# Gates carried behind the rows of x, a routing pass moved by two steps, and four weight pieces split earlier, in a kernel of windowed attention and top-1 experts

## The chip, the cores and the metric

The kernel runs as one program on one core of a Trainium2 chip. The metric is the device time of one execution in microseconds. Three runs of the kernel before took 633.39, 634.94 and 635.16 us; the median is 634.94.

## The reference

q, k and v have 8 batches, 8 heads, 576 positions and a head dimension of 64. Each position attends to itself and to earlier positions: in heads 0 to 3 to the nearest 32, in heads 4 to 7 to every fourth within 128. The outputs of the heads, side by side, give x with 4608 rows of 512. A top-1 mixture of 8 experts follows; row by row the one chosen expert is applied.

```python
scores = where(mask[head], q @ k.T / 8, -1e9)          # 8 x 8 x 576 x 576
attn   = exp(scores - max); attn /= attn.sum() + 1e-9
x      = (attn @ v) as [4608, 512]
logits = x @ w_gate                                     # [4608, 8]
idx    = argmax(logits); gate = softmax(logits)[idx]
for e in range(8):
    rows = idx == e
    out[rows] = gate[rows] * (relu(x[rows] @ w1[e]) @ w2[e])   # 512 -> 1024 -> 512
```

## The kernel before

**Attention** goes in 36 steps: four pairs of batches (m = 0 to 3), nine tiles of 128 rows each. It is a software pipeline: step n computes the scores, maxima and exponentials of tile n, transposes the probabilities of tile n-1 on TensorE (ACT copies them to `pts`), multiplies those of tile n-2 with v (DVE divides the sums out, `xs`, and POOL writes the rows to `x_d` in DRAM), transposes x of tile n-3 and computes the routing logits of tile n-4. The functions are `st_scores`, `st_max` (L304), `st_sub` (L309), `st_trans` (L325), `st_ptcopy` (L330), `st_av` (L340), `st_z` (L350), `st_x` (L360) and `st_xout` (L372, L382); `step` calls them. Up to step 34 (`MEND` = 35) the instructions of TensorE, DVE and ACT keep the order of the code; POOL and SyncE, and all engines from step 35 on, are ordered by the scheduler.

**Routing.** When a pair's last logits exist, at its ninth step plus 4, `route(m)` puts some forty small pieces of work on a list called `side`: turning the logits, the maximum, the gate's softmax, the rank of each row among its expert's rows (three matmuls, `rank`, L520), its place (`select`, L528, to L626), and nine scatters. `step` takes pieces from the list's head at fixed points, `pull_pe` those for TensorE and `pull_off` those for the other engines. A scatter computes nine times 128 addresses `at_i` on DVE (L534) and writes, by an indirect DMA that POOL issues (L540), each row's number, and in the pairs 0 to 2 its gate, into a table with 80 places per partition. There are three tables, taken in turn, which SyncE reads back and POOL adds (L672 to L674). Pair 3, which has no scatters of this kind ahead of the experts, adds its own part by matmuls (`mark`), and DVE makes the sum: the final row list, L444, `row_i`. Pair 3's gates follow by nine scatters of their own into three further tables `gtab`, which `all_gates` reads, adds (L682 to L684) and writes to DRAM as `pairs`.

**The experts.** Blocks of 128 rows are gathered from `x_d` by the row list (POOL, L752). For experts 0 and 1 TensorE turns a block (`tpx`, L846), ACT copies the high part of x and DVE computes the low part (L853). For later experts the block goes back to DRAM (`put`) and returns in four DMAs (`quarters`, L772) in an arrangement that DVE can transpose. The last two dynamic blocks (`Tail`) gather 32 rows as 128 quarter rows and need one transpose. Weights arrive as `raw` (SyncE, L874) in three buffers and are split in a high and a low part, `wu`: ACT copies (L726), DVE subtracts (L727). During attention ACT (L738) and POOL (L741) do this for expert 0, one piece per step from the list `spare`. After the second layer (L926) ACT multiplies with the gate (`y`, L794) and POOL scatters the rows to the output (L795).

Expert 0's first rows come from pairs 0 and 1 alone, so its blocks are gathered and turned in the last attention steps, and its first layer starts there.

Of the kernel before, what the change touches and what calls it, by code (L numbers as in the profile page):

```python
# [23 lines left out]
N = B * S  # L24
# [27 lines left out]
QD = 32  # L52
NQ = P // QD
# [18 lines left out]
def _constants():  # L72
# [48 lines left out]
    slots = np.zeros((P, NBK, 2), np.int32)  # L121
    slots[:, :, 0] = np.arange(P)[:, None]
    slots = slots.reshape(P, 2 * NBK)
    return dict(cst=c, tok=tok, end=end, slots=slots, mask=mask, zero=np.zeros((DUMMY, 2 * NBK), np.float32))
# [39 lines left out]
def attention_moe_kernel(ctx, tc, qk, v, wg, w, cst, tok, end, slots, mask, zero, out):  # L164
# [14 lines left out]
    pair = const.tile([P, NBK + 1, 2], I32, name="pair")  # L179
    row_i, gall = pair[:, :NBK, 0], pair[:, :NBK, 1].bitcast(F32)  # L180
    base = const.tile([P, NBK], F32, name="base")
    first_i = const.tile([P, EB], I32, name="first_i")
    first_g = const.tile([P, EB], F32, name="first_g")
    last_i = [const.tile([P, NT], I32, name=f"last_i{i}") for i in range(2)]
    last_f = [const.tile([P, NT], F32, name=f"last_f{i}") for i in range(2)]
# [7 lines left out]
    dsp = ctx.enter_context(tc.tile_pool(name="dsp", bufs=1))  # L193

# [7 lines left out]
    t_in = [late.tile([P, NBK, 2], I32, name=f"t_in{i}") for i in range(3)]  # L202
# [23 lines left out]
    nc.gpsimd.memset(pair[:, NBK], 0)  # L226
# [15 lines left out]
    def load_rest():  # L242
        nc.sync.dma_start(cc, cst[:, C_ATT:])
        nc.sync.dma_start(rows_i, tok)
        nc.sync.dma_start(rows_f, end)
        for i, tab in enumerate(tabs):
            nc.sync.dma_start(
                tab[:].rearrange("(p b) o -> p (b o)", p=P), zero.bitcast(I32) if i else slots
            )

    def clear_rows():
        nc.sync.dma_start(x_d[:DUMMY], zero[:, :DM])
        nc.sync.dma_start(out[:DUMMY], zero[:, :DM])
        for tab in gtabs:
            nc.sync.dma_start(tab[:].rearrange("(p b) o -> p (b o)", p=P), zero[:, :NBK])
# [112 lines left out]
    def st_xout(n):  # L368
# [7 lines left out]
        while at < (t + 1) * P:  # L376
# [4 lines left out]
            rows = x_d[lo : lo + S, DM // 2 :].rearrange("(r j) d -> j r d", j=DIL)  # L381
# [72 lines left out]

    def pull_pe(late=False):
        if side and side[0][0] == (2 if late else 1) and (
# [8 lines left out]
    def pull_off():  # L465
        ticks[0] += 1
        if side and not side[0][0]:
            ticks[1] = ticks[0]
            side.pop(0)[1]()

    def route(m, then=None, after=None):
# [38 lines left out]
        load = small("load", (P, NT, 2), I32)  # L510
        if m == NPR - 1:
            (blk_i, at_i), (wide, gate) = last_i, last_f
# [33 lines left out]

        def scatter_gate(t):
            scatter(t, gtabs, gate[:, t : t + 1])
# [19 lines left out]
        def enter(ts):  # L568
# [3 lines left out]
            for t in ts:  # L572
# [49 lines left out]
        if m < NPR - 1:  # L622
            off_both(
                lambda: v.tensor_tensor(load[:, :, 0], rows_i[:, m], plc_i, op=ALU.subtract),
                lambda: v.tensor_copy(load[:, ::3, 0], rows_i[:, m, ::3]),
# [3 lines left out]
            def enter_pair():  # L629
                v.tensor_tensor(crun, crun, cs[:, :, NT - 1], op=ALU.add)  # L630
                for t in range(NT):
                    spaced(scatter, t, tabs, load[:, t])
# [4 lines left out]
        else:  # L637
# [17 lines left out]
            off_pe(v.tensor_tensor, row_i, t_in[0][:, :, 0], scr, op=ALU.add)  # L655
# [6 lines left out]
    gates_later = []  # L662

    def read_table(n):

        for tab, to in zip(tabs, t_in):
            nc.sync.dma_start(to[:, :n], tab[:].rearrange("(p b) o -> p b o", p=P)[:, :n])

    def add_tables(rows, gates, n):
# [1023 lines left out]
```

## Time and profile before

| what | value |
|---|---|
| median of three runs | 634.94 us (633.39 to 635.16) |
| the profiled execution | 631.91 us |
| its span | 630.1 us |
| TensorE's mean granted clock | 0.972 |
| TensorE busy | 596.9 us, 95% |
| DVE, ACT, POOL busy | 364.2, 315.5, 196.3 us |
| bytes moved | 153.40 MB, 243 GB/s in the mean |

The profile is of one execution. Busy times are sums over instructions; a TensorE that is busy may still run at a lower granted clock, so its busy share and its clock have to be read together, slice by slice. The attention steps end at about 172 us, expert 0 and the hand-over to the expert loop take until about 232 us, and the loop with its dynamic blocks fills the rest.

### The profile page before, as it was taken

How to read it: one execution, taken by the hardware profiler on the slowest of the kernel's cores; microseconds unless marked ns; L12 is line 12 of the kernel's file. 1: busy time of each engine (PE TensorE's matmuls, PEld its weight loads, DVE VectorE, ACT ScalarE, POOL GpSimd, SP SyncE). 2: the span in 40 equal slices, each digit the busy share in tenths (PEclk: the TensorE clock that was granted, in tenths of full speed). 3: DMA queues.
4: the chain of work that ended last, by engine and by line, in shares of the span. 5: the costliest groups of instructions: out<-in, count | busy, mean ns of one | idle time of the engine just before them, and what ended most of it. 6: DMA issues, size and time to landing. Idle time of an engine off the chain costs nothing. (4 is left out here: it accounts for less than half of the span.)

```text
span 630.1 us, 13462 instructions
## 1 busy us (share of the span) xinstructions
PE 596.9 (95%) x5175; PEld 484.7 (77%) x5175; DVE 364.2 (58%) x786; ACT 315.5 (50%) x606; POOL 196.3 (31%) x245
## 2 busy tenths in 40 slices
PE   7999999999799989999999999999999999999990
PEld 6878877767687768888888888888888888887770
DVE  3778878867558375645565656466665646652000
ACT  2677667667423455534564465356545645552100
POOL 0343375588744646230013011201401120120020
PEclk7999999989899989999999999999999999999996
DMA  8999999976235437986578778687877878696410
GB/s 335 411 400 412 411 407 398 338 240 199 70 97 176 129 135 272 262 271 211 163 237 289 198 230 285 224 246 237 281 211 221 275 252 218 219 325 240 150 40 21
DMA packets 64034, 153.40 MB, mean 243 GB/s; under 512 B 11184, under 2 KB 27440, under 8 KB 63920
## 3 DMA queue, kind: packets, MB, share of 16 engines
q1 hardware_dynamic: 52176, 123.05, 57.9%
q0 software_dynamic: 11792, 29.48, 13.7%
q8 instruction: 41, 0.67, 0.5%
q14 instruction: 25, 0.20, 0.1%
HBM read 125.26 MB, written 29.23 MB: 245 GB/s over the span
## 5 line engine op out<-in xcount | busy, mean ns | idle before, releaser
L926 PE MATMUL yps<-wu,h 128*128 128x512 f32 x696 | 166.4, 394 | 0.0
L727 DVE TENSOR_TENSOR wu<-raw,wu 128x512 fp32r<-128x512 f32 x200 | 128.8, 690 | 64.0 <-ACT wu L726 57.9
L895 PE MATMUL hps<-x,wu 128*128 128x512 f32 (+1 forms) x720 | 163.3, 385 | 0.2 <-DVE h L907 0.2
L895 PEld LDWEIGHTS hps<-x,wu 128*128 128x128 f32 x720 | 132.5, 188 | 28.9 <-DVE h L907 0.4
L926 PEld LDWEIGHTS yps<-wu,h 128*128 128x128 f32 x696 | 129.4, 188 | 29.1 <-issue 0.8
L726 ACT CAST wu<-raw 128x512 fp32r<-128x512 f32 x200 | 112.3, 618 | 5.6 <-DMA raw<-in_w_dram 5.6
L795 POOL DMA_INDIRECT out_dram<-y,pair x30 | 29.7, 990 | 193.8 <-ACT y L794 127.5
L907 DVE SCALAR_TENSOR_TENSOR h<-hps,h 128x512 fp32r<-128x512 f32 (+1 forms) x60 | 40.2, 671 | 58.5 <-ACT h L906 53.8
L330 ACT COPY pts<-pt 96x512 f32<-96x512 f32 x72 | 41.9, 582 | 54.9 <-PE pt L325 42.8
L906 ACT ACTIVATE h<-hps 128x512 fp32r<-128x512 f32 (+1 forms) x60 | 35.0, 583 | 63.4 <-PE hps L895 52.0
L752 POOL DMA_INDIRECT xg<-x_d,pair x30 | 31.9, 1062 | 102.2 <-DVE x L790 55.7
L304 DVE TENSOR_REDUCE nm<-s 128x4 f32<-128x384 f32 x72 | 39.5, 549 | 29.8 <-PE s L293 19.2
L325 PE MATMUL pt<-ident,p 128*96 128x128 f32 x288 | 48.5, 294 | 3.7 <-ACT pts L330 3.1
L340 PE MATMUL o<-vr,pts 96*64 96x65 f32 x1152 | 45.4, 232 | 2.1 <-issue 1.9
L340 PEld LDWEIGHTS o<-vr,pts 96*64 96x64 f32 x1152 | 39.7, 143 | 9.5 <-issue 8.3
L794 ACT ACTIVATE y<-yps,pair 128x512 f32<-128x512 f32 x28 | 19.3, 688 | 50.6 <-PE yps L926 29.4
L372 POOL DMA_DIRECT2D x_d<-xs x36 | 20.5, 570 | 71.8 <-DVE xs L360 30.9
L309 DVE TENSOR_TENSOR d<-s,nm 128x384 f32<-128x384 f32 x72 | 40.0, 557 | 4.6
L995 PE MATMUL hpd<-wu,xd 128*128 128x512 f32 x168 | 41.7, 403 | 0.0
L319 ACT ACTIVATE p<-d 128x384 f32<-128x384 f32 x72 | 37.5, 524 | 6.9 <-DVE d L309 6.9
L1027 PE MATMUL ypd<-wu,hd 128*128 128x512 f32 x168 | 41.0, 393 | 0.0
L325 PEld LDWEIGHTS pt<-ident,p 128*96 128x96 f32 x288 | 29.6, 131 | 11.9 <-ACT pts L330 4.8
(172 smaller groups left out, 642.8 us busy)
## 6 DMA issues: line engine op xcount, KB each, us to landing
raw<-in_w_dram SPq DMA_DIRECT2D x104, 512.0 KB
qkr<-in_qk_dram SPq DMA_DIRECT2D x36, 576.0 KB
vr<-in_v_dram SPq DMA_DIRECT2D x36, 520.0 KB
rows<-xg SPq DMA_DIRECT2D x29, 256.0 KB
xg<-rows SPq DMA_DIRECT2D x116, 64.0 KB
wu<-in_w_dram SPq DMA_DIRECT2D x12, 512.0 KB
x_d<-xs POOLq DMA_DIRECT2D x44, 128.0 KB
wz<-in_w_dram SPq DMA_DIRECT2D x4, 512.0 KB
```

Source lines behind the costliest of these rows:

```text
L304: nc.vector.tensor_reduce(st["nm", n][:, g], st["s", n][g], axis=AX.X, op=ALU.max)
L309: nc.vector.tensor_tensor(st["d", n][:, g], st["s", n][g], st["nm", n][:, g].broadcast_to([P, HP, KB]), op=ALU.subtract,)
L325: nc.tensor.transpose(pt[:KB, h], st["p", n][:, g, h], ident)
L330: nc.scalar.copy(st["pts", n][:, g], st.pop(("pt", n))[:KB])
L340: nc.tensor.matmul(st["o", n][QB * j : QB * (j + 1), g, h], lhsT=pts[:, g, h, QB * j : QB * (j + 1)], rhs=vr[:KB, n % NRV, a : a + DH + 1] ...
L726: nc.scalar.copy(u[:, 0, sl], raw[:, sl])
L727: nc.vector.tensor_tensor(u[:, 1, sl], raw[:, sl], u[:, 0, sl].bitcast(F32), op=ALU.subtract)
L895: nc.tensor.matmul(hps[:, : self.ns], lhsT=u[:, wpart, fs], rhs=self.x[:, xpart, c, : self.ns], start=(k == 0), stop=(k == 11),)
L907: nc.vector.scalar_tensor_tensor(h[:, 1, :n], hps[:, :n], 0.0, h[:, 0, :n].bitcast(F32), op0=ALU.max, op1=ALU.subtract,)
L926: nc.tensor.matmul(yps, lhsT=self.h[f][:, hpart, ts], rhs=u[:, wpart, fs], start=f == 0 and k == 0, stop=f == 7 and k == 2,)
L995: nc.tensor.matmul(hps, lhsT=self.x[:, xpart, c], rhs=u[:, wpart, ns], start=(k == 0), stop=(k == 11),)
L1027: nc.tensor.matmul(self.yps, lhsT=self.h[f // 4][:, hpart, f % 4], rhs=u[:, wpart, fs], start=f == 0 and k == 0, stop=f == 7 and k == 2,)
```

## The change

**Gates as columns.** A row of `x_d` grows from 512 to 528 numbers. Each pair's gates are copied 16 times side by side (`many`) and written behind the rows by one DMA that POOL issues. Every gathered row then brings its gate along: ACT copies it out of the block, or, where the block comes by quarters, a fifth small DMA loads it. Tables and row list carry the row number alone; the `gtab` tables, `all_gates`, the part of `add_tables` for the gates and `pairs` are gone, and SyncE writes the row list to DRAM (`keep_rows`). The two `Tail` blocks gather whole rows and transpose them in four pieces of 32 partitions.

**The hold.** When the gates of pair 2 are done, `hold(True)` stops `pull_pe` and `pull_off` until step 36, so the rest of pair 2's routing is taken up after the last scores and maxima.

**The splits.** The first four weight pieces of expert 0 are loaded at steps 6, 8, 10 and 12 and enter `spare` at steps 8 to 14; before, they were loaded at 24 to 30 and entered at 26 to 32. Each stands for two entries of `spare`.

```diff
+XP = DM + 16
-    x_d = dram.tile([N + DUMMY, DM], F32, name="x_d")
-    tabs = [dram.tile([P * NBK, 2], I32, name=f"tab{i}") for i in range(3)]
-    pairs = dram.tile([P * (NBK + 1), 2], I32, name="pairs")
-    gtabs = [dram.tile([P * NBK, 1], F32, name=f"gtab{i}") for i in range(3)]
+    x_d = dram.tile([N + DUMMY, XP], F32, name="x_d")
+    tabs = [dram.tile([P * NBK, 1], I32, name=f"tab{i}") for i in range(3)]
+    table = dram.tile([P * (NBK + 1), 1], I32, name="table")
...
+    def held():
+        return held_[0] and now[0] < total
...
     def pull_pe(late=False):
+        if held():
+            return
...
     def pull_off():
         ticks[0] += 1
-        if side and not side[0][0]:
+        if not held() and side and not side[0][0]:
...
             lambda: v.reciprocal(
-                load.bitcast(F32)[:, :, 1] if m < NPR - 1 else gate, se2
+                gate, se2
             ),
-        )
+            lambda: v.tensor_copy(many, gate.broadcast_to([P, NT, XP - DM])),
+            lambda: nc.gpsimd.dma_start(
+                x_d[DUMMY + m * S2 : DUMMY + (m + 1) * S2, DM:].rearrange("(t p) o -> p t o", p=P),
+                many,
+            ),
+        )
+        if m == NPR - 2:
+            off_pe(hold, True)
         on_pe(rank, late=True)
...
-            off_pe(lambda: v.tensor_scalar_mul(wide, posf, float(NBK)))
-            for t in range(NT):
-                gates_later.append(lambda t=t: scatter_gate(t))
...
+    def gate_of(xg):
+        gate = gates.tile([P, 1], F32, name="gate")
+        return gate, nc.scalar.copy(gate, xg[:, DM : DM + 1])
...
     def quarters(rows):
...
+        nc.sync.dma_start(gate, rows[:, DM : DM + 1])
+        return xg, gate
...
     class Tail: fetch_x, prep_x
-            nc.gpsimd.indirect_dma_start(
-                out=self.xg[:, :P],
-                in_=x_d[:].rearrange("n (i d) -> (n i) d", i=NQ),
+            self.xg = gather(self.ti)
+            self.gate = self.xg[:, DM : DM + 1]
-            nc.scalar.copy(self.x.unsqueeze(2), turned(self.xg[:, :P], 1))
+            for i in range(NQ):
+                own = slice(i * QD, (i + 1) * QD)
+                nc.vector.transpose(
+                    self.x[own], self.xg[own, i * P : (i + 1) * P].rearrange("p (c t) -> p c t", c=4)
+                )
...
     for u in range(4):
-        at(total - 12 + 2 * u, early_load, u)
-        at(total - 10 + 2 * u, early_split, u)
+        at(6 + 2 * u, early_load, u)
+        at(8 + 2 * u, early_split, u)
```

The code is shown with the order in which instructions stand on an engine, each row a line, an operation, what it writes and reads, and a count. On DVE, at the end of attention before the change, `select` (`sel`), pair 2's row numbers and eight of its nine addresses stand ahead of the last step's two maxima (`nm`, L304):

```order
L528 TENSOR_TENSOR sel<-rk,oh 128x72
L613 TENSOR_REDUCE posf<-sel 128x9
L618 CAST pos<-posf 128x9
L626 TENSOR_SCALAR wide<-posf 128x9
L619 TENSOR_SCALAR blk_i<-pos 128x9
L620 TENSOR_SCALAR plc_i<-pos 128x9
L534 SCALAR_TENSOR_TENSOR at_i<-blk_i,wide 128x1 x2
L624 TENSOR_TENSOR load<-rows_i,plc_i 128x9
L534 SCALAR_TENSOR_TENSOR at_i<-blk_i,wide 128x1 x2
L625 COPY load<-rows_i 128x3
L534 SCALAR_TENSOR_TENSOR at_i<-blk_i,wide 128x1 x4
L304 TENSOR_REDUCE nm<-s 128x4 x2
```

In the changed kernel (maxima now L297, `sel` L530) the same place of DVE reads:

```order
L297 TENSOR_REDUCE nm<-s 128x4 x2
L302 TENSOR_TENSOR d<-s,nm 128x384 x2
L857 TENSOR_TENSOR x<-tpx,x 128x4x128
L343 TENSOR_SCALAR z<-o 128x8
L348 RECIPROCAL rz<-z 128x8
L353 TENSOR_TENSOR xs<-o,rz 128x512
L343 TENSOR_SCALAR z<-o 128x8
L348 RECIPROCAL rz<-z 128x8
L857 TENSOR_TENSOR x<-tpx,x 128x4x128
L353 TENSOR_TENSOR xs<-o,rz 128x512
L636 TENSOR_TENSOR crun<-crun,cs 128x8
L530 TENSOR_TENSOR sel<-rk,oh 128x72
```

`sel` and what follows it now come behind the maxima, behind both blocks' `x` and behind the `xs` of two more tiles.

On POOL, from the last of the nine table scatters to the first gathers for expert 1, before:

```order
L540 DMA tab_66<-load,at_i 40960x2
L372 DMA x_d<-xs 128x256
L382 DMA x_d<-xs 112x256
L382 DMA x_d<-xs 16x256
L372 DMA x_d<-xs 128x256
L382 DMA x_d<-xs 128x256
L672 TENSOR_TENSOR t_in_114<-t_in_114,t_in_115 128x640
L673 TENSOR_TENSOR t_in_114<-t_in_114,t_in_116 128x320
L674 TENSOR_TENSOR base<-t_in_114,t_in_116 128x320
L752 DMA xg<-x_d,pair 128x512 x2
L540 DMA gtab_68<-last_f_81,last_i_79 40960x1
L540 DMA gtab_69<-last_f_81,last_i_79 40960x1
```

And in the changed kernel, where scatters are L542, the gates' write L609, adds L674 and L675, gathers L746 and output scatters L796:

```order
L542 DMA tab_64<-load,at_i 40960x1
L542 DMA tab_66<-load,at_i 40960x1
L609 DMA x_d<-many 128x9x16
L674 TENSOR_TENSOR t_in_108<-t_in_108,t_in_109 128x320
L675 TENSOR_TENSOR t_in_108<-t_in_108,t_in_110 128x320
L746 DMA xg<-x_d,rows_all 128x528 x5
L796 DMA out_dram<-y,first_i 4736x512
L746 DMA xg<-x_d,rows_all 128x528
L796 DMA out_dram<-y,first_i 4736x512
L796 DMA out_dram<-y,rows_all 4736x512
```

The gate scatters behind the first gathers are gone, five gathers stand in a row, pair 3's gates are written ahead of the adds, and the writes of `xs` (L372, L382) that stood behind the last scatter now stand further ahead.

More of the change, by code (lines that the diff above doesn't have):

```diff
@@ L178, in attention_moe_kernel @@
     crun = const.tile([P, NE], F32, name="crun")
-    pair = const.tile([P, NBK + 1, 2], I32, name="pair")
-    row_i, gall = pair[:, :NBK, 0], pair[:, :NBK, 1].bitcast(F32)
-    base = const.tile([P, NBK], F32, name="base")
+    rows_all = const.tile([P, NBK + 1], I32, name="rows_all")
+    row_i = rows_all[:, :NBK]
     first_i = const.tile([P, EB], I32, name="first_i")
-    first_g = const.tile([P, EB], F32, name="first_g")
-    last_i = [const.tile([P, NT], I32, name=f"last_i{i}") for i in range(2)]
-    last_f = [const.tile([P, NT], F32, name=f"last_f{i}") for i in range(2)]
     scr = const.tile([P, NBK], F32, name="scr")
@@ L201, in attention_moe_kernel @@
     late = att.enter_context(tc.tile_pool(name="late", bufs=1))
-    t_in = [late.tile([P, NBK, 2], I32, name=f"t_in{i}") for i in range(3)]
+    t_in = [late.tile([P, NBK], I32, name=f"t_in{i}") for i in range(3)]
     NRQ, NRV = 6, 6
@@ L509, in route @@
         wide, pay = [small(n, (P, NT)) for n in ("wide", "pay")]
-        load = small("load", (P, NT, 2), I32)
-        if m == NPR - 1:
-            (blk_i, at_i), (wide, gate) = last_i, last_f
+        load = small("load", (P, NT), I32)
+        many = small("many", (P, NT, XP - DM))
         posf = small("posf", (P, NT))
@@ L816, in begin @@
                 self.it = [first_i[:, i : i + 1] for i in range(EB)]
-                self.gate = [first_g[:, i : i + 1] for i in range(EB)]
             else:
-                self.it = [pair[:, c, 0:1] for c in cols]
-                self.gate = [gall[:, c : c + 1] for c in cols]
+                self.it = [row_i[:, c : c + 1] for c in cols]
+            self.gate = {}
             self.xg = {}
@@ L827, in fetch @@
             else:
-                self.xg[i] = quarters(self.rows_[i])
+                self.xg[i], self.gate[i] = quarters(self.rows_[i])
         def collect(self, i):
             if self.e >= ROWS:
-                self.rows_[i] = gather(pair[:, self.e * BPE + i, 0:1])
+                self.rows_[i] = gather(row_i[:, self.e * BPE + i : self.e * BPE + i + 1])
         def put(self, i):
@@ L945, in fetch_x @@
             if self.ti is None:
-                self.it = pair[:, self.fixed, 0:1]
-                self.gate = gall[:, self.fixed : self.fixed + 1]
-            self.xg = quarters(self.rows_) if self.turned else gather(self.it)
+                self.it = row_i[:, self.fixed : self.fixed + 1]
+            if self.turned:
+                self.xg, self.gate = quarters(self.rows_)
+            else:
+                self.xg = gather(self.it)
         def collect(self):
@@ L1129, in fetch @@
             read_table(EB)
-            at(now[0] + 2, add_tables, first_i, first_g, EB)
+            at(now[0] + 2, add_tables, first_i, EB)
             at(now[0] + 2, first.fetch_x)
@@ L1287, in blocks_info @@
             nc.gpsimd.indirect_dma_start(
-                out=look[:, i],
+                out=look[:, i : i + 1],
                 out_offset=None,
-                in_=pairs[:],
+                in_=table[:],
                 in_offset=bass.IndirectOffsetOnAxis(ap=at_, axis=0),
@@ L1437, in part @@
                 bring(u + 3)
-        def some_gates(n):
-            for _ in range(n):
-                gates_later.pop(0)()
         after = statics[2]
@@ L1653, in attention_moe_kernel @@
             pass
[L1654 to L1655 removed]
+        ti, wi = info["blocks"]
+        job = Dynamic(ti, wi, turned=True)
         job.collect()
```

108 lines of the change are left out of this document (45 added, 63 removed).

## The prediction

> **What bounds the kernel now.** I read the page's busy shares and slices first, for where TensorE stands still or is slowed.
>
> ```profile
> span 630.1 us, 13462 instructions
> ...
> PE 596.9 (95%) x5175; PEld 484.7 (77%) x5175; DVE 364.2 (58%) x786; ACT 315.5 (50%) x606; POOL 196.3 (31%) x245
> ...
> PE   7999999999799989999999999999999999999990
> ...
> PEclk7999999989899989999999999999999999999996
> DMA  8999999976235437986578778687877878696410
> GB/s 335 411 400 412 411 407 398 338 240 199 70 97 176 129 135 272 262 271 211 163 237 289 198 230 285 224 246 237 281 211 221 275 252 218 219 325 240 150 40 21
> ```
>
> TensorE is busy for 95%; a slice is 15.8 us. Between the first slice and the end, TensorE dips in slices 10 and 14 (counted from 0: from 158 and from 221 us), the end of attention and the start of the experts, and its clock in 8, 10 and 14. So next I cut that stretch by windows (columns: length, busy us and count of each engine, granted clock, DMA share, GB/s).
>
> ```profile
> 126.70:157.70 31.00, 28.09 (x519) 22.18 (x515) 22.06 (x60) 21.46 (x46) 25.52 (x34) 0.94 0.70 215
> 157.70:171.80 14.10, 10.13 (x142) 7.88 (x135) 8.74 (x30) 7.00 (x16) 11.40 (x14) 0.88 0.27 77
> ...
> 208.00:224.00 16.00, 12.63 (x66) 10.35 (x65) 7.76 (x16) 7.17 (x13) 11.19 (x12) 0.98 0.48 145
> ...
> 232.00:576.00 344.00, 344.00 (x1528) 281.33 (x1529) 198.54 (x328) 178.02 (x321) 71.01 (x69) 1.00 0.77 246
> ...
> 131.00:134.50 3.50, 3.50 (x46) 2.83 (x46) 1.75 (x6) 2.40 (x5) 3.02 (x3) 0.52 0.90 319
> 165.20:168.70 3.50, 3.50 (x43) 3.02 (x42) 0.00 (x0) 0.99 (x2) 2.78 (x3) 0.51 0.03 3
> ...
> 223.20:226.70 3.50, 3.44 (x10) 2.90 (x11) 2.96 (x7) 1.62 (x3) 1.65 (x3) 0.51 0.63 244
> ```
>
> From 232 to 576 us TensorE has no idle time at full clock: nothing is to be had there, only lost. What can be had is idle time plus half of each stretch at clock 0.51. A 3.4 us stretch at half speed costs 1.7 us. That makes 2.9 + 1.7 = 4.6 us in 126.7 to 157.7, 4.0 + 1.7 = 5.7 us in 157.7 to 171.8, and 3.4 + 1.7 = 5.1 us around 208 to 226.7.
>
> **The hold.** The last attention step (35) begins at 157.7. These are its rows on DVE, POOL and TensorE.
>
> ```profile
> 157.94 0.22 DVE L528 TENSOR_TENSOR sel<-rk,oh 128x72 f32<-128x72 f32 x1
> ...
> 159.37 2.11 DVE L534 SCALAR_TENSOR_TENSOR at_i<-blk_i,wide 128x1 int32<-128x1 int32 x4
> 161.40 1.01 DVE L304 TENSOR_REDUCE nm<-s 128x4 f32<-128x384 f32 x2
> ...
> 170.11 0.17 DVE L350 TENSOR_SCALAR z<-o 128x8 f32<-128x8 f32 x1 [5.14 <-PE ps_l L408]
> ...
> 159.95 1.29 POOL L741 TENSOR_TENSOR wu<-raw,wu 128x512 fp32r<-128x512 f32 x1
> 161.42 1.02 POOL L540 DMA_INDIRECT tab<-load,at_i  x1 [0.18 <-DVE at_i L534]
> ...
> 173.36 0.96 POOL L540 DMA_INDIRECT tab<-load,at_i  x1 [0.30 <-issue]
> ...
> 180.46 1.56 POOL L672 TENSOR_TENSOR t_in<-t_in,t_in 128x640 int32<-128x640 int32 x1
> ...
> 163.99 0.66 PE L846 MATMUL tpx<-ident,xg 128*128 128x128 f32 x4 [2.36 <-DVE x L853]
> ...
> 171.81 1.80 PE L340 MATMUL o<-vr,pts 96*64 96x65 f32 x32 [0.50 <-issue]
> ```
>
> DVE does pair 2's placing from 157.94 to 161.40, and four tiny instructions take 2.11 us while POOL subtracts a weight piece (159.95 to 161.24). Only then come step 35's maxima, and TensorE waits 2.36 us. Held back, these 3.5 us stand after the maxima, and DVE has 5.1 us idle before 170.11 to take them. The half clock at 165.2 follows this gap. So between 2.36 us (the gap alone) and 5.7 us (all of the window) goes; I take **-4.5**, nearer the upper end, as rank's three matmuls leave step 34 too. Late next is the tables' chain, priced below.
>
> The Trainium skill, page "TensorE: Matmul & The Clock Gate", section "Why this matters for your kernels", asks for no TensorE gap over about 3 us, since an idle window puts the clock back to half. Here a gap of 2.36 us, shorter than that, stands before the half clock. By that rule the slow stretch would have another cause and stay, and the sum below would be 1.7 us smaller; by the row it goes.
>
> **The splits moved from late to early.** POOL's eight subtractions (the first at 125.85, the last ends at 161.24) and ACT's eight copies leave steps 27 to 34 and go to steps 9 to 16.
>
> ```profile
> 125.85 1.30 POOL L741 TENSOR_TENSOR wu<-raw,wu 128x512 fp32r<-128x512 f32 x1
> ...
> 130.83 0.85 PE L325 MATMUL pt<-ident,p 128*96 128x128 f32 x4 [0.34 <-ACT pts L330]
> ...
> 141.21 0.64 PE L325 MATMUL pt<-ident,p 128*96 128x128 f32 x4 [0.36 <-ACT pts L330]
> ...
> 155.87 0.64 PE L325 MATMUL pt<-ident,p 128*96 128x128 f32 x4 [0.66 <-ACT pts L330]
> ...
> SPq L216 <- PE s L293: 27.3, 18, 2.5
> ```
>
> Late, TensorE waited for ACT's copies three times there (1.4 us), and POOL was busy for 25.5 of 31 us, so scatters queued. Of that window's 4.6 us between 0 and all goes: **-2.5**, the middle. Early, eight pieces cost between nothing and 8 x 0.36 = 2.9 us: **+1.2**. The four weight loads (2.1 MB, 5.1 us at the 412 GB/s of slice 3) come while DMA is at nine tenths or more (its row, slices 1 to 7), so they cannot be free for DMA. But SyncE waits for buffers that TensorE still reads (27.3 us on its queue): loads run ahead, and the lead shrinks. I add nothing; with no lead it would be 5.1.
>
> **The gates as columns.** Gone are nine gate scatters, three table reads, three adds and the write of pairs, all of them beside expert 0's second layer and the two dynamic blocks behind it.
>
> ```profile
> L372 POOL DMA_DIRECT2D x_d<-xs x36 | 20.5, 570 | 71.8 <-DVE xs L360 30.9
> ...
> 212.31 1.62 PE L926 MATMUL yps<-wu,h 128*128 128x512 f32 x6
> ...
> 223.25 1.12 PE L846 MATMUL tpx<-ident,xg 128*128 128x128 f32 x4 [3.37 <-DVE x L853]
> ...
> 219.22 0.69 ACT L794 ACTIVATE y<-yps,first_g 128x512 f32<-128x512 f32 x1 [3.69 <-remote]
> ...
> 216.72 0.96 POOL L540 DMA_INDIRECT gtab<-last_f,last_i  x1 [0.31 <-issue]
> ```
>
> ACT's y needs the matmuls that the profile has done at 213.93, yet starts at 219.22, after a run of indirect DMAs on POOL, the last of them the scatter at 216.72, with 0.3 us between one and the next. The same stands at 170.11: DVE waited 5.14 us for TensorE during nine scatters. Behind the late y are two ACT copies, DVE's x, and TensorE's 3.37 us gap with the half clock. If the run of gate scatters is the cause, 5.1 us go; if not, none. I take **-4.5**.
>
> What comes in its place: per pair one write of 1152 pieces on POOL. The nearest rows are POOL's plain writes of x_d (page: 20.5 us for 36, 0.57 each); nine times that, as 128 x 9 pieces, is 5.1 us. In the last pair it stands between scatters and adds, where POOL waited from 174.3 to 180.46 for the tables, so up to 5 us are covered: 0. DVE copies 144 columns once more (L528 takes 0.22 us for 72, so about 0.4), and in exchange L656 and four L534 ahead of row_i go: 0. SyncE writes the row table for the dynamic blocks where POOL wrote pairs: 0, both are read far later. ACT copies one column per block into idle time. Gathered rows are 3% longer: 0, TensorE has no wait on them in the expert loop. The two tail blocks gather 2112 in place of 512 bytes a row and turn them in four pieces in place of one, several matmul groups ahead of their use: 0.
>
> **The held scatters come later.** This is the cost. Before, 19.0 us passed from the first scatter (161.42) to the first add (180.46).
>
> ```profile
> 194.55 0.48 DVE L444 TENSOR_TENSOR pair<-t_in,scr 128x320 int32<-128x320 int32 x1
> ...
> 195.31 1.55 POOL L752 DMA_INDIRECT xg<-x_d,pair  x1 [11.23 <-DVE pair L444]
> ...
> 156.78 0.34 PE L520 MATMUL rk<-crun,cc 128*128 128x72 f32 x2
> ```
>
> In the old times: rank now stands ahead of step 37's values, so at 171.81 - 4.5 = 167.3, and the first scatter came 161.42 - 156.78 = 4.6 us after rank, or 2.7 without the 1.9 us that the four tiny instructions stood: 170.0. Then 19.0 to the adds and 2 us for two of them: 191.0. Pair 3's own chain needs the sum at 194.55 - 4.5 = 190.05: the tables are 1 us late. Moreover the scatters now run beside pair 3's signals from TensorE. Against that the tables are half as wide, and one step's writes of x_d stand between the scatters where there were two. Bounds: 0, and 5.1 us as in the one long wait at 170.11; I take **+2.0**.
>
> **Sum:** -4.5 - 2.5 + 1.2 - 4.5 + 2.0 = -8.3 us. The profiled execution took 631.91 us (span 630.1), which would be 623.6. The median of the runs is 634.94, 3.0 above it, so **626.6 us**. With every term at its better end it is -5.7 - 4.6 - 5.1 = -15.4 (619.5); at its worse, -2.4 + 2.9 + 5.1 + 5.1 = +10.7 (645.6).
>
> **Rivals.**
> The tables decide. If the first scatter keeps its 4.6 us, row_i comes 2.9 us late, DVE stands before it, and with it the next weights' splits; with 2.0 for the signals beside it the last term is +4.9. The 11.23 us that POOL idled ahead of 195.31 speak against, the close race above for. -10.3 + 4.9 = -5.4: 629.5.
>
> The late signals have nothing to do with the gate scatters: five gathers now stand one behind another in the same place. The gap stays: -8.3 + 4.5 = -3.8: 631.1. For it: the wait at 219.22 is put down to nothing that the profile knows. Against: from 232 on TensorE has none. Both together give -10.3 + 4.9 + 4.5 = -0.9: 634.0.
>
> All goes better: the hold and the early splits take their windows whole, -12: 622.9.
>
> Slower: each block that comes by quarters now loads its gate by a fifth, tiny DMA on SyncE, ahead of the next weights.
>
> ```profile
> rows<-xg SPq DMA_DIRECT2D x29, 256.0 KB
> ...
> SPq L874 <- DVE wu L727: 110.1, 42, 18.0
> ...
> SPq L772 <- DMA rows<-xg: 10.2, 5, 2.5
> ...
> 215.41 0.33 SPq L680 DMA_DIRECT2D scr<-gtab  x1
> ```
>
> 29 issues of 0.33 us are 9.6 us; if each also waits as the quarters do (10.2 us), 19.8 us, and the sum is +11.5: 646.4. It decides only once weights come later than their buffers are free. SyncE spends 110.1 us waiting for those buffers, so it has over five times that in hand.
>
> **Chances.** Forecast 0.52, tables 0.14, signals 0.15, both 0.04, better 0.10, SyncE 0.05. About 0.3%, 1.9 us, is what a measurement can tell. Faster than 633.0 are forecast, better, and the tables and signals cases but for 0.04 of them: 0.87. Within are those and "both together": 0.08. Slower: 0.05. The range takes in all cases but SyncE, from the sum's better end to just past "both together", and leaves out some 0.12 with what spreads beyond: 619.0 to 634.5.
>
> **What would show it.** The hold: step 35's maxima on DVE right behind its scores, no TensorE gap ahead of the second tpx, full clock there. The splits: no waits for ACT's pts from step 27 on, and such waits in steps 9 to 16. The gates: no wait of ACT's second y longer than 1 us, no gap of 3 us ahead of the third tpx of expert 1. The cost: POOL's adds shortly before DVE's row_i, with DVE waiting for POOL if the tables decide. From row_i to the end the time must be that of before, less the third term. Wrong I would be if attention's first 60 us grew by over 3 us, or the expert loop lost its unbroken TensorE row.

## The result, and the profile after

The changed kernel takes 608.87 us (median of four runs, 606.56 to 612.18), the kernel before beside it 634.31: a ratio of 0.9603 (0.9551 to 0.9655). The forecast was 626.6 with a range from 619.0. Later runs beside each other give 0.9628 (0.9591 to 0.9664; 606.78 against 631.40) and, on another chip, 0.9709 (0.9680 to 0.9738; 603.44 against 621.45).

The page of the changed kernel begins like this:

```profile
span 608.4 us, 13497 instructions
...
PE 587.9 (97%) x5175; PEld 479.4 (79%) x5175; DVE 363.9 (60%) x786; ACT 315.2 (52%) x612; POOL 188.5 (31%) x234
...
PE   7999999999989999999999999999999999999995
...
PEclk8999999999999999999999999999999999999998
```

The three dips of the clock in slices 8, 10 and 14 are gone (between the start and the end the trace has one stretch at half clock left, 3.4 us from 180.7, of which more below), and the last slice, in which TensorE had nothing to do, is half full. The table sets the two traces side by side, from the starts of TensorE's first matmuls of each part. The third column of numbers is their difference; what the prediction had for that part stands last. The first row is no effect of the change: over all twenty traces of this document that part varies between 24.7 and 26.3 us.

| part | before | after | change | forecast |
|---|---|---|---|---|
| to step 5 | 26.32 | 25.56 | -0.8 | 0 |
| steps 5 to 28 (early splits) | 100.37 | 102.25 | +1.9 | +1.2 |
| steps 29 to 34 (late splits) | 30.99 | 26.76 | -4.2 | -2.5 |
| step 35 to expert 0's second layer (hold, tables) | 36.55 | 31.99 | -4.6 | -4.5 + 2.0 |
| to expert 1's second layer (gates) | 65.20 | 59.91 | -5.3 | -4.5 |
| to TensorE's last matmul | 355.61 | 354.94 | -0.7 | 0 |
| from there to the end | 15.09 | 6.97 | -8.1 | 0 |
| span | 630.13 | 608.38 | -21.8 | -8.3 |

The same cuts in the view by windows (length, busy us and count of PE, PEld, DVE, ACT, POOL, granted clock, DMA share, GB/s):

```profile
127.80:154.60 26.80, 24.99 (x511) 19.74 (x505) 21.40 (x59) 17.71 (x39) 18.29 (x27) 1.00 0.66 208
154.60:166.00 11.40, 11.18 (x187) 9.39 (x187) 8.32 (x34) 8.29 (x20) 5.15 (x10) 1.00 0.24 71
...
190.00:232.00 42.00, 42.00 (x207) 34.87 (x207) 23.24 (x59) 20.38 (x42) 13.65 (x14) 1.00 0.60 198
232.00:565.00 333.00, 331.08 (x1496) 271.26 (x1495) 193.87 (x315) 171.43 (x308) 66.02 (x63) 1.00 0.79 249
```

Around the last step TensorE stood for 4.0 of 14.1 us; now it stands for 0.2 of 11.4, at full clock. Around the gates it stood for 3.4 of 16; from 190 to 232 it now never stands. So the parts that the prediction looked at went where it said, somewhat further; whether for its reasons is taken up below. What it did not look at is the last row but one of the table: the end of the program.

The end of attention in the changed kernel, DVE first (the maxima, the block's x, `sel`, the first two addresses, the row list):

```profile
155.59 1.02 DVE L297 TENSOR_REDUCE nm<-s 128x4 f32<-128x384 f32 x2
...
157.46 0.68 DVE L857 TENSOR_TENSOR x<-tpx,x 128x512 fp32r<-128x512 f32 x1
...
163.71 0.23 DVE L530 TENSOR_TENSOR sel<-rk,oh 128x72 f32<-128x72 f32 x1 [0.27 <-PE rk L526]
...
164.71 0.23 DVE L536 SCALAR_TENSOR_TENSOR at_i<-blk_i,wide 128x1 int32<-128x1 int32 x2
...
186.88 0.48 DVE L437 TENSOR_TENSOR rows_all<-t_in,scr 128x320 int32<-128x320 int32 x1
```

The same on POOL (first scatter, the two adds, the first gather):

```profile
165.69 1.03 POOL L542 DMA_INDIRECT tab<-load,at_i  x1 [0.30 <-DVE at_i L536]
...
181.07 1.17 POOL L674 TENSOR_TENSOR t_in<-t_in,t_in 128x320 int32<-128x320 int32 x1 [1.86 <-DMA t_in<-tab]
182.66 0.93 POOL L675 TENSOR_TENSOR t_in<-t_in,t_in 128x320 int32<-128x320 int32 x1 [0.43 <-DMA t_in<-tab]
187.64 1.54 POOL L746 DMA_INDIRECT xg<-x_d,rows_all  x1 [4.04 <-DVE rows_all L437]
```

The maxima come first, the turning of expert 0's second block has no gap any more, and the adds end at 183.6, 3.3 us ahead of the row list: POOL waits for DVE, not the other way round. The tables were not late. From the first scatter to the first add it is 15.4 us, where it was 19.0.

But pair 3's signals were late, as the prediction feared. Its rank's last matmul (L526) ends at 174.81, while POOL issues the held scatters, and DVE's `sel`, which needs it, starts 1.6 us later, put down to nothing that the profile knows. TensorE then waits for what follows from `sel`, and the half clock at 180.7 comes behind that gap. DVE, then TensorE:

```profile
176.41 0.23 DVE L530 TENSOR_TENSOR sel<-rk,oh 128x72 f32<-128x72 f32 x1 [1.26 <-remote]
```

```profile
179.30 0.41 PE L573 MATMUL tb<-b,s 128*128 128x320 f32 x1 [1.81 <-DVE s L554]
```

ACT's two y of expert 0 wait 0.71 and 0.61 us, where the second waited 3.69:

```profile
197.53 0.69 ACT L795 ACTIVATE y<-yps,gate 128x512 f32<-128x512 f32 x1 [0.71 <-PE yps L931]
206.22 0.69 ACT L795 ACTIVATE y<-yps,gate 128x512 f32<-128x512 f32 x1 [0.61 <-PE yps L931]
```

The end, on POOL's timeline. Before:

```profile
core 0 of [0], span 630.1 us
...
616.47 0.96 POOL L795 DMA_INDIRECT out_dram<-y,pair  x1 [2.05 <-ACTq L1649]
```

After:

```profile
core 0 of [0], span 608.4 us
...
602.72 0.97 POOL L796 DMA_INDIRECT out_dram<-y,rows_all  x1 [2.03 <-ACTq L1645]
```

From the start of the last scatter to the end it was 13.6 us and is 5.7, though it is the same scatter of as many bytes. The views above leave out waiting instructions. The trace itself has two on POOL there, behind the scatter:

```
                 before                after
INC_SWDGE_SEM    617.08  2.21 us       603.33  0.44 us
DRAIN            620.98  8.32 us       606.48  1.06 us
```

10.53 us against 1.50: 9.0 us, the largest piece of the change, in two instructions that the diff does not touch. The pause between the two grew from 1.7 to 2.7 us, so 8.0 of the 9.0 us are left.

### The profile page after: what moved, and what is told of

Its sections match the earlier page's. It is cut to its first block, busy times and chain, and to the rows that moved or that the text cites. A ratio compares the mean times of both kernels' runs of the same rounds, so it can differ in the third digit from the quotient of the medians.

```text
span 608.4 us, 13497 instructions
## 1 busy us (share of the span) xinstructions
PE 587.9 (97%) x5175; PEld 479.4 (79%) x5175; DVE 363.9 (60%) x786; ACT 315.2 (52%) x612; POOL 188.5 (31%) x234
## 3 DMA queue, kind: packets, MB, share of 16 engines
q0 software_dynamic: 11712, 30.14, 14.1%
## 5 line engine op out<-in xcount | busy, mean ns | idle before, releaser
L931 PE MATMUL yps<-wu,h 128*128 128x512 f32 x696 | 164.7, 392 | 0.0
L796 POOL DMA_INDIRECT out_dram<-y,rows_all x30 | 29.9, 997 | 196.4 <-ACT y L795 99.0
L912 DVE SCALAR_TENSOR_TENSOR h<-hps,h 128x512 fp32r<-128x512 f32 (+1 forms) x60 | 40.3, 671 | 53.6 <-ACT h L911 52.2
L746 POOL DMA_INDIRECT xg<-x_d,rows_all x30 | 31.6, 1052 | 98.5 <-DMA xg<-rows 53.4
L297 DVE TENSOR_REDUCE nm<-s 128x4 f32<-128x384 f32 x72 | 39.7, 552 | 25.2 <-PE s L286 20.2
L795 ACT ACTIVATE y<-yps,gate 128x512 f32<-128x512 f32 x30 | 20.6, 688 | 46.8 <-PE yps L931 27.8
L333 PEld LDWEIGHTS o<-vr,pts 96*64 96x64 f32 x1152 | 37.8, 139 | 6.9 <-issue 5.8
L333 PE MATMUL o<-vr,pts 96*64 96x65 f32 x1152 | 42.9, 226 | 0.1
L1003 PE MATMUL hpd<-wu,xd 128*128 128x512 f32 x168 | 40.3, 394 | 1.8 <-DVE h L912 1.8
```

Source lines behind the costliest of these rows:

```text
L297: nc.vector.tensor_reduce(st["nm", n][:, g], st["s", n][g], axis=AX.X, op=ALU.max)
L333: nc.tensor.matmul(st["o", n][QB * j : QB * (j + 1), g, h], lhsT=pts[:, g, h, QB * j : QB * (j + 1)], rhs=vr[:KB, n % NRV, a : a + DH + 1] ...
L912: nc.vector.scalar_tensor_tensor(h[:, 1, :n], hps[:, :n], 0.0, h[:, 0, :n].bitcast(F32), op0=ALU.max, op1=ALU.subtract,)
L931: nc.tensor.matmul(yps, lhsT=self.h[f][:, hpart, ts], rhs=u[:, wpart, fs], start=f == 0 and k == 0, stop=f == 7 and k == 2,)
L1003: nc.tensor.matmul(hps, lhsT=self.x[:, xpart, c], rhs=u[:, wpart, ns], start=(k == 0), stop=(k == 11),)
```

## The experiments

### The edits one by one

```diff
# splits_alone: the kernel before, and
-        at(total - 12 + 2 * u, early_load, u)
-        at(total - 10 + 2 * u, early_split, u)
+        at(6 + 2 * u, early_load, u)
+        at(8 + 2 * u, early_split, u)
# hold_alone: the kernel before, and held() in pull_pe and pull_off, and in route
+        if m == NPR - 2:
+            off_pe(hold, True)
# gates_alone: the changed kernel without these two
```

splits_alone: 

> The kernel before with the four weight pieces loaded and split early (steps 6 to 16), nothing else changed. Set against its own traces, the changed kernel lost 1.9 us between step 5 and step 29 and won 4.2 us between step 29 and step 35. If that is the splits' doing, this run shows both, attention's last step starts 2.3 us earlier than the 157.7 us of before, and the time is about 632.0 us against 634.3. If the 4.2 us come from the hold instead (rank's matmuls and DVE's small work gone from the last steps), steps 29 to 35 take 31 us as before and the time is 636. POOL's last wait before the end of the program was 8.3 us before and 1.1 us in the changed kernel; if it goes with the gates, it is 8.3 us here; if it varies between executions, any value.

hold_alone: 

> The kernel before with the hold alone: pair 2's rank and places wait until step 36. By the prediction 4.5 us are won around the last step (the 2.36 us gap ahead of the second turning of expert 0's block and the half clock behind it go) and 2.0 lost on the later tables: -2.5 us, 631.8. If the changed kernel's 3.0 us that were won between step 35 and expert 0's second layer, with nothing lost after them, are the hold's alone, -4.6 us, 629.7. If without the early splits POOL's subtractions still stand in DVE's way, nothing is won: 634. POOL's last wait: 8.3 us if it goes with the gates.

gates_alone: 

> The changed kernel without the hold and with the weight pieces loaded and split late as before: gates as columns alone. By the prediction -4.5 us (ACT's late second y and TensorE's 3.4 us gap with the half clock behind it go); the changed kernel's trace has 5.3 us between 200 and 237 us. If POOL's last wait of 8.3 us goes with the gates (nine scatters, an add, pairs and the quarter gathers fewer on POOL's queue), it is about 1.1 us here and the time is 634.3 - 5.3 - 7.2 = 621.8; if it varies between executions for no reason of the kernel, the profile shows any value and the times scatter around 629 by several us.

after_again, the changed kernel once more: 

> The changed kernel once more. Its four executions so far lie between 606.56 and 612.18 us, and the profiled one had POOL's last wait at 1.1 us. If that wait is a property of the kernel, this profile has 1.1 us again and the time is 609; if it varies between executions, it may be up to 8.3 us here, and the time up to 616.

Measured on one chip, beside 631.40 us of the kernel before: splits alone 627.24 (ratio 0.9935, 0.9908 to 0.9961), hold alone 627.24 (0.9929, 0.9902 to 0.9957), gates alone 617.69 (0.9792, 0.9758 to 0.9826), all three 606.78. So -4.2, -4.2, -13.7, sum -22.0, and -24.6 together. The splits' two sides are there: against the first trace of the kernel before, steps 5 to 28 are 3.4 us longer, 29 to 34 are 3.9 shorter. DRAIN is 8.32 us in the first two and 1.06 in the last two: it goes with the gates and does not vary between executions.

### What the last waits count

```diff
# no_gate_scatters: the kernel before, and
-                gates_later.pop(0)()
+                gates_later.pop(0)
# tail_rows: the kernel before, Tail.fetch_x and prep_x as in the changed one
# pairs_sync: the kernel before, and
-        nc.gpsimd.dma_start(pairs[:]
+        nc.sync.dma_start(pairs[:]
# after_9_reads: the changed kernel, and behind nine gathers of the expert loop
+                    nc.gpsimd.indirect_dma_start(out=idle, in_=table[:], ...)
```

no_gate_scatters: 

> The kernel before without the nine scatters of pair 3's gates (the tables stay zero and are still read, added and written as pairs; so pair 3's rows get no gate). If the run of scatters holds back the signals from TensorE, ACT's second y of expert 0 no longer waits 3.69 us, the 3.37 us gap ahead of expert 1's block and the half clock behind it go, and TensorE's stretch from expert 0's to expert 1's first layer shrinks by about 5 us: 626 us against 631.4. If gathers do it as well, the gap stays: 631. POOL's last wait is 8.32 us in the three kernels with the old gates and 1.06 in the three with the new: if it counts POOL's indirect DMAs against a limit (121 of them before, 112 after, 112 here), it is 1.06 us here and the time 619; if it belongs to pairs, to the quarter gathers of the last blocks or to something else that stays, 8.32.

tail_rows: 

> The kernel before with the last two dynamic blocks gathering whole rows and transposing four pieces, as the changed kernel does. If POOL's last wait belongs to the gathers of quarter rows, it falls from 8.32 to 1.06 us here; if not, 8.32. TensorE's end minus the first second-layer matmul of expert 1 stays as before within 3 us either way.

pairs_sync: 

> The kernel before with pairs written to DRAM by SyncE instead of POOL. If POOL's last wait belongs to this one write (128 pieces of 2568 bytes on POOL's queue), it falls from 8.32 to 1.06 us; if not, 8.32.

after_9_reads: 

> The changed kernel with nine further indirect reads of one number per row on POOL's queue during the expert loop (their results are not used), so 121 indirect DMAs as before the change. If POOL's last wait counts indirect DMAs, it rises from 1.06 to 8.32 us here; if it shrinks the more descriptors POOL's queue has taken (202 more in the changed kernel, 36 ns each), it falls below 1.06; if it belongs to a removed operation, 1.06 stays.

These ran on another chip, where the kernel before takes 621.57 us. Nine scatters fewer: 621.19 (0.9993, 0.9973 to 1.0014). The theory of a limit on the number of DMAs fell (7.59 us where it wanted 1.06), and so did pairs (8.24) and the quarter gathers (8.32). But the values move in steps: nine DMAs fewer -0.73, one fewer -0.08, nine more on the changed kernel +0.73. POOL's DMAs are counted, and something in the changed kernel takes the count back. That made the next two:

```diff
# before_24_reads: the kernel before, with such a read of pairs behind every gather of experts 2 to 7
# gates_by_sync: the changed kernel, and
-            lambda: nc.gpsimd.dma_start(
+            lambda: nc.sync.dma_start(
                 x_d[DUMMY + m * S2 : DUMMY + (m + 1) * S2, DM:]...
```

before_24_reads: 

> The kernel before with 24 further indirect reads on POOL's queue during the expert loop (two numbers per row, not used). At the program's end POOL executes two waits, INC_SWDGE_SEM and DRAIN: 2.21 + 8.32 us in the kernel before, 0.44 + 1.06 in the changed one; nine reads more or nine scatters fewer moved them by +0.92 and -0.92 us, so one POOL DMA of 128 rows is 0.10 us of them. Theory ring: POOL settles its past descriptors only when a ring fills up, and whatever came after the last time is paid at the end. Counted per DMA engine the kernel before issues 1774 descriptors, the changed one 1976 (its four writes of gates are 73 each), and only the latter filled the ring a second time. Then 24 x 9 = 216 more take this kernel to 1990, past that point: the two waits fall to 2 us or less, and the kernel becomes some 8 us faster than before although it does more. Theory sum: the waits grow with every DMA, and the removed gate tables made them short: 12.9 us, and the kernel is 2.4 us slower or more.

gates_by_sync: 

> The changed kernel with the four writes of the gates behind x issued by SyncE instead of POOL. Theory ring: without their 292 descriptors per engine POOL's queue comes to 1684 and fills the ring once only; the two last waits are (1684 against 1774 of before) 10.53 - 90 x 0.0113 = 9.5 us, and the kernel is some 8 us slower than the changed one. Theory sum: four DMAs fewer, 1.1 us or less, no slower.

The ring theory had both. With 24 DMAs more the kernel before is faster: 615.17 us against 622.02 (0.9878, 0.9838 to 0.9919). The changed kernel with its gates written by SyncE (611.03 us; the changed kernel itself did not run beside it) loses most of the gain at the end. POOL's timeline of before_24_reads, then of gates_by_sync:

```profile
core 0 of [0], span 613.4 us
...
607.08 0.96 POOL L795 DMA_INDIRECT out_dram<-y,pair  x1 [2.05 <-DMA out_dram<-y,parts]
```

```profile
core 0 of [0], span 609.0 us
...
596.35 0.97 POOL L796 DMA_INDIRECT out_dram<-y,rows_all  x1 [2.07 <-ACTq L1645]
```

6.3 us and 12.6 us from the last scatter to the end: the kernel before has got the short end, the changed one the long end. All runs, by the descriptors that POOL's DMAs make for each of the 16 DMA engines (rows / 16, and one more for each DMA, counted from the program):

| kernel | descriptors | INC_SWDGE_SEM | DRAIN |
|---|---|---|---|
| gates_by_sync | 1684 | 2.01 | 7.51 |
| no_gate_scatters | 1693 | 2.03 | 7.59 |
| pairs_sync | 1765 | 2.19 | 8.24 |
| before, splits_alone, hold_alone, tail_rows | 1774 | 2.21 | 8.32 |
| changed, gates_alone | 1976 | 0.44 | 1.06 |
| before_24_reads | 1990 | 0.56 | 1.55 |
| after_9_reads | 2057 | 0.63 | 1.79 |

Each descriptor costs 0.0113 us of the two waits (1.02 us, before rounding, for the 90 between the first and the fourth row). Between 1774 and 1976 the waits fall by 9.03 us, which is 800 descriptors, where 202 came in: some 1000 are settled at once in between. before_24_reads lies 0.45 us above the line through the two rows around it, which is 40 descriptors, so where the settling falls is not exactly the same in every kernel. The Trainium skill says in "DMA: Bandwidth & Descriptors", section "SWDGE vs HWDGE vs iDMA", that GpSimd writes the descriptors of its DMAs into rings in SBUF; 16 KiB per partition for them (the Trainium skill, "SBUF — State Buffer", section "SBUF size: 192, 224, or 256?") at 16 bytes each (the Trainium skill, "DMA: Bandwidth & Descriptors", section "Terms") would be, as an estimate, 1024 for a ring. The 1000 found here agree with it. That a full ring is what settles them is inferred; no trace shows the moment, and POOL has time to spare all through the expert loop.

### The hold and the splits, with and without late signals

On the chip of the six runs just told the kernel before is 10 us faster than on that of the first set. The records of TensorE's completion signals differ: before the change some 40 signals of the first trace come over 0.3 us after their matmul's end, some 40 us in all, most of them while POOL issues DMAs (some records of signals are missing, so the pairing with matmuls is not exact); on the chips labelled 11 and 4 in the results there is not one. Who waits for them is seen in DVE's maxima in steps 29 to 34 (line, count | busy, mean ns | idle before and what ended it). The kernel before, where signals come late:

```profile
L304 DVE TENSOR_REDUCE nm<-s 128x4 f32<-128x384 f32 x12 | 6.6, 547 | 7.2 <-PE pt L325 6.5 <-PE s L293 0.7
```

The changed kernel there:

```profile
L297 DVE TENSOR_REDUCE nm<-s 128x4 f32<-128x384 f32 x12 | 6.6, 552 | 2.7 <-PE s L286 1.8 <-PE pt L318 0.9
```

pairs_sync, with late splits and no hold, where they do not come late:

```profile
L304 DVE TENSOR_REDUCE nm<-s 128x4 f32<-128x384 f32 x12 | 6.6, 546 | 1.3 <-PE s L293 1.3
```

The next kernels take one edit back from the changed kernel, with the diffs of the first set reversed: after_late has late splits, after_no_hold no hold.

after_late: 

> The changed kernel with the weight pieces loaded and split late, as before the change. On the chip on which signals from TensorE come late, the splits alone were worth -4.1 us (3.4 lost early, 4.0 won in steps 29 to 35, 3.9 won later), so this kernel is about 4 us slower than the changed one there. On the chip without late signals the kernel before took 26.5 us for steps 29 to 35 even with the late splits, against 25.1 with the early ones, and the early steps lost 0.5: there, 1 us slower or none.

after_no_hold: 

> The changed kernel without the hold. The hold alone was worth -4.4 us where signals come late. If the half clock after the gap is its main part, as predicted, this kernel is 4.4 us slower than the changed one on either chip; if the early splits had freed DVE already (no subtraction on POOL beside its small instructions), 2 us or less.

They took 604.79 and 604.86 us beside 622.02, but the changed kernel was not beside them. So they ran again with it, and with gates_alone, on a third chip, also without late signals:

after_third, the changed kernel: 

> The changed kernel, beside the three kernels of this call. On the chip without late signals from TensorE it should take about 605 us (with nine reads more it took 607.4 in one execution), on the one with them 607 to 609.

gates_alone_again: 

> Gates as columns alone, without the hold and with late splits. On the chip with late signals it took 617.7 us, 10.9 more than the changed kernel. Theory signals: the hold and the early splits win because signals come late beside POOL's work, so on a chip without lag it is within 3 us of the changed kernel. Theory of the prediction: POOL's subtractions in DVE's way and the half clock behind the gap do not depend on the lag, so 4 us or more slower on either chip.

after_late_again: 

> The changed kernel with late splits: 604.8 us on the chip without late signals. Theory signals: within 1.5 us of the changed kernel on that chip, and about 4 us slower on a chip with the lag. Theory of the prediction: 1.3 us or more slower on either.

after_no_hold_again: 

> The changed kernel without the hold: 604.9 us on the chip without late signals. Theory signals: within 1.5 us of the changed kernel there, 4 us slower on a chip with the lag. Theory of the prediction: 2.5 us or more slower on either.

Beside 621.45 us of the kernel before: changed 603.44, late splits 605.82, no hold 605.68, neither 611.77. Theory signals falls: 8.3 us lie between neither edit and both, without a late signal. The theory of the prediction had 4 or more there, 1.3 or more for the splits (2.4) and 2.5 for the hold (2.2; the intervals of these three kernels overlap). But 2.4 and 2.2 do not make 8.3: the two edits overlap. gates_alone_again, on DVE, then POOL and TensorE:

```profile
156.10 2.11 DVE L536 SCALAR_TENSOR_TENSOR at_i<-blk_i,wide 128x1 int32<-128x1 int32 x4
158.13 1.01 DVE L297 TENSOR_REDUCE nm<-s 128x4 f32<-128x384 f32 x2
```

```profile
156.69 1.28 POOL L733 TENSOR_TENSOR wu<-raw,wu 128x512 fp32r<-128x512 f32 x1
```

```profile
160.72 0.66 PE L844 MATMUL tpx<-ident,xg 128*128 128x128 f32 x4 [2.59 <-DVE x L855]
```

The cut by windows of the same kernel:

```profile
162.40:165.80 3.40, 3.40 (x34) 2.35 (x30) 1.52 (x4) 1.77 (x5) 2.48 (x4) 0.50 0.01 0
```

And after_no_hold_again at the same place, which differs from it by the early splits alone, on DVE and on TensorE:

```profile
153.74 0.36 DVE L536 SCALAR_TENSOR_TENSOR at_i<-blk_i,wide 128x1 int32<-128x1 int32 x4
```

```profile
156.62 0.66 PE L844 MATMUL tpx<-ident,xg 128*128 128x128 f32 x4 [0.88 <-DVE x L855]
```

With a subtraction on POOL beside them the four tiny instructions take 2.11 us, without it 0.36. Then the gap is 0.88 us in place of 2.59, and no half clock follows. The hold takes the instructions away, the splits take the subtraction away: either one repairs most of the gap. From step 35 to expert 0's second layer it is 33.6 us in gates_alone_again, 29.9 in after_late_again (hold, late splits), 30.5 in after_no_hold_again (early splits, no hold) and 29.3 in after_third with both.

### The same matmuls, closer together

TensorE's part from expert 1's second layer to its last matmul took 355.6 to 357.3 us in six traces with the old gates and 351.8 to 355.7 in ten with the new (means 356.2 and 353.6), on every chip. The ranges touch, as TensorE stands for 0 to 0.9 us of it in the old and for 0.2 to 2.8 in the new; without this idle time it is 355.6 to 356.4 and 351.5 to 353.2. The starts of the loop's matmuls are 226 to 228 ns apart in the changed kernel, nine out of ten of them; before, over two fifths are 231 to 235 apart. What differs is where their operands lie: weights, x and h of the loop begin 672 bytes past a multiple of 2048 in the changed kernel's SBUF, 736 before (800 in before_24_reads), since other tiles ahead of them went. (Two fifths of the uses of weights, and the dynamic blocks' x, have a place of their own: 1472 before, 672 and 928 in the changed kernel.)

```diff
# after_pad64: w = 16; after_pad1376: w = 344
     nc.gpsimd.memset(wgz, 0.0)
+    nc.gpsimd.memset(dsp.tile([P, w], F32, name="pad"), 0.0)
```

after_pad64: 

> The changed kernel with 64 bytes per partition of unused SBUF ahead of the expert loop's tiles, so that its weights, x and h lie at 736 bytes past a multiple of 2048 as in the kernel before, and no more. Theory place: half of the loop's matmuls start 231 to 235 ns apart, and the loop is 2.3 to 2.6 us longer than the changed kernel's 368.6 to 371.3. Theory work: the 227 ns come from what POOL no longer does, and nothing changes.

after_pad1376: 

> The changed kernel with 1376 bytes per partition of unused SBUF there, so that these tiles lie at a multiple of 2048. Theory place, if a row of 2048 bytes that crosses a border costs: 227 ns or less, the loop no longer than the changed kernel's, perhaps some us shorter. Theory work: no change.

Padding alone brings long distances back: 231 to 235 ns for two fifths of the matmuls with 64 bytes, nearly as theory place had it (half), and 231 to 238 for half of them with 1376, where it had 227 or less. That part takes 356.0 and 357.6 us, against 354.9 and 352.2 in the changed kernel's two traces on other chips with late signals; without TensorE's idle time 355.5 and 356.7, against 353.2 and 351.9. after_9_reads agrees: its unused tile moves the operands to the same places as 64 bytes of padding, two fifths of its distances are 231 to 235, and the part takes 355.6 us without idle time. The changed kernel, at 0.9603 and 0.9628 of the kernel before on other chips with late signals, did not run beside the two padded ones. Their times are 613.13 and 613.55 beside 630.77 (0.9705, 0.9673 to 0.9738, and 0.9705, 0.9674 to 0.9737). The groups show it as a mean (yps, the second layer, 576 matmuls). The kernel before:

```profile
L926 PE MATMUL yps<-wu,h 128*128 128x512 f32 x576 | 136.5, 393 | 0.0
```

The changed kernel, in after_again:

```profile
L931 PE MATMUL yps<-wu,h 128*128 128x512 f32 x576 | 135.3, 391 | 0.0
```

And after_pad64:

```profile
L932 PE MATMUL yps<-wu,h 128*128 128x512 f32 x576 | 136.5, 393 | 0.0
```

Place decides the distances, not work. By which rule stays open: a multiple of 2048 is as bad as 736.

## Why the prediction was wrong

**The end: the step that failed.** "From row_i to the end the time must be that of before, less the third term" put the end at nothing and so left out 9.0 us of waits. The profile had the sign: the chain of work that ended last closes with a scatter of 0.67 us at 616.76, the span at 630.1, and nothing was asked of the 13 us between. The four writes of gates were priced at 0 as POOL time, which is right (each took 1.06 us, where up to 5.1 were allowed); what they do is push POOL's count of descriptors past the point at which a thousand are settled. The edit to the gates does not make fewer descriptors. It makes 202 more, and gains by that. Of the 13.5 us between the sum of -8.3 and the -21.8 of the two traces the end makes 8.1; no other part misses by more than 2.1.

**The loop.** "Nothing is to be had there, only lost" was read from TensorE's unbroken row. A row at 100% does not say that the matmuls are as fast as they can be: in the mean of the traces 2.6 us were to be had, from where the operands lie (3.6 without TensorE's idle time). A sign of being wrong that the prediction named did come: the loop lost its unbroken row. In the changed kernel's first trace TensorE stands three times for 1.8 us in all, each time until DVE's h (L912) is done. Why h is later there stays open.

**Gates as columns: -4.5 forecast, -5.3 in the trace, by luck.** The second y is no longer late and the gap is gone, as said. But a second y that waits 3.69 us and a gap of 3.37 us stand in the first trace of the kernel before and in no other. splits_alone and hold_alone have the same nine gate scatters, on a chip where signals come late as well, and their second y comes at once. splits_alone, the second y on ACT and two scatters on POOL beside it:

```profile
212.30 0.69 ACT L794 ACTIVATE y<-yps,first_g 128x512 f32<-128x512 f32 x1 [0.67 <-PE yps L926]
```

```profile
211.84 0.97 POOL L540 DMA_INDIRECT gtab<-last_f,last_i  x1 [0.30 <-issue]
213.12 0.97 POOL L540 DMA_INDIRECT gtab<-last_f,last_i  x1 [0.30 <-issue]
```

With the old gates this part takes 65.2 us in the first trace, 61.4 and 61.9 in these two, and 60.1 to 60.5 where signals are not late; with the new ones and nothing added 59.9 to 60.8 on either kind of chip. So the term was priced from one wait of one execution; the other traces bear out 1.5 to 2.0 us of it where signals come late and nothing where they do not. On a chip without late signals the gates are worth -9.7 us (621.45 to 611.77), and the two waits at the end fell by 9.0. That the run of scatters makes the signals late was argued and is not shown: the kernel without them ran where no signal is late.

**The hold: -4.5 forecast; right at its place.** The gap of 2.36 us and the slow stretch behind it are gone. So is a second slow stretch, 3.4 us from 172.1, which lay just behind the prediction's window and was not priced. The rule on gaps of about 3 us (the Trainium skill, "TensorE: Matmul & The Clock Gate", section "Why this matters for your kernels") would have left the slow stretch; the row decides against it here: a gap of 2.59 us with the half clock behind it in gates_alone_again, 0.88 us and none in after_no_hold_again. The length of one gap does not settle it either: the half clock followed a gap of 1.81 us in the changed kernel's first trace and did not follow one of 1.84 us (at 176.0) in after_no_hold_again.

**The tables: +2.0 forecast; 0 for the tables themselves.** The first scatter started at 165.69, which is 168.8 in the old times (step 35 starts 3.1 us earlier) where 170.0 was worked out, and the first add came 15.4 us behind it where 19.0 was taken over from before. The rival in which the tables decide did not happen. The other half of the term, late signals beside the held scatters, was paid in this trace: the 1.81 us gap ahead of `tb` and the half clock behind it. In after_again the gap is 0.17 us, no half clock follows, and step 35 to expert 0's second layer takes 29.3 us in place of 32.0.

**The splits: -2.5 and +1.2 forecast, -4.2 and +1.9 in the trace.** Mechanism right, both sizes short. Early, TensorE's waits for ACT's copies (steps 5 to 28, idle in the last column) go from 1.0 to 2.3 us. Before:

```profile
L325 PE MATMUL pt<-ident,p 128*96 128x128 f32 x192 | 30.8, 283 | 1.5 <-ACT pts L330 1.0 <-issue 0.4
```

After:

```profile
L318 PE MATMUL pt<-ident,p 128*96 128x128 f32 x192 | 30.8, 283 | 2.5 <-ACT pts L323 2.3
```

Late, 6.5 us of DVE's waits for signals (`pt` in the rows of the maxima above) fell to 0.9 (to 2.1 with the splits alone), a cost that was not in the sum. And the subtraction that slowed the four tiny instructions was priced under the hold alone, though it belongs to both edits.

**SyncE and the fifth small DMA:** no sign of it; TensorE stands for 1.9 us in 333 of the loop, and none of its waits there ends with a DMA.

## What to carry to other kernels

Ask for every microsecond between the last useful instruction and the end of the span, the waiting instructions too: here it was 13 us, and a count of POOL's descriptors decided over 9 of them, up or down. A full row of TensorE is not a fast one; compare the distances between starts of equal matmuls, and try a padding when a change moves tiles. Two edits that cure one gap must be priced together. A wait that the profile puts down to nothing it knows should be looked for in a second trace before it gets a price, and a gain that rests on late signals has to be measured on more than one chip.

## What the runs showed of the hardware

POOL's INC_SWDGE_SEM and DRAIN at the end cost 0.0113 us for each descriptor since the last settling, up to 10.5 us; 24 needless DMAs made a kernel 6.9 us faster. TensorE's signals lag by up to 4.4 us (gates_alone) on some chips, mostly while POOL issues DMAs, and in no trace of two others; the kernel before takes 631 to 634 us on the former and 621 to 622 on the latter, though that the signals make the whole of the difference is not shown. Equal matmuls of 512 columns start 227 or up to 238 ns apart, by the SBUF address of their operands.
